# Handing out an expert's four row gathers at once instead of in separate chore slots

## The chip, the cores and the metric

The kernel runs on one core of one Trainium2 chip. The metric is the device time of one execution in microseconds (us); the times given are medians of several executions. A core has five engines, each with a queue of its own, which holds its instructions in the order in which the program emitted them: TensorE (PE in the profile, its weight loads PEld) multiplies matrices, VectorE (DVE) and ScalarE (ACT) work on tiles, GpSimd (POOL) does both some tile work and the indirect DMAs, and SyncE (SP) only issues DMAs. An instruction waits on semaphores for what it needs, and everything behind it in its queue waits with it.

## What is computed

Attention with a sigmoid in place of the softmax, and behind it a mixture of eight experts in which each of 3584 tokens goes to one expert, 448 tokens to each:

```python
scores = q @ k^T / sqrt(64) - log(448);  attn = sigmoid(scores);  x = attn @ v     # 8 x 12 heads, 448 tokens
# routing: the 3584 x 8 logits x @ w_gate in falling order; a token is given to the
# expert of its largest logit that still has room (448 places each)
for e in range(8):
    h = maximum(x[mask_e] @ w1[e], 0)      # 768 -> 1024
    out[mask_e] = h @ w2[e]                # 1024 -> 768
```

## The kernel before, in words

The first part (to about 275 us) computes attention and logits and writes the rows x to a scratch tensor `xs` in HBM. The rest is the eight experts, one after the other. Which expert comes at which step is found by the routing, so "expert 0" to "expert 7" here are steps 0 to 7, not indices of weights.

**Routing** (`Router`, L118 and on). For each step VectorE finds by a 16-step search (L177, 16 steps of about 2 us) the threshold of the next expert to fill, and builds the list of its 448 tokens in `r_idx` (L297). It is a Python generator that emits a piece of itself at each `next(route)`; the list of a step is known to the program as `listed[kx]`. The list of step kx + 1 is built while the expert of step kx multiplies; the routing runs a little faster than the experts, so the lists come earlier and earlier in their expert's predecessor.

**An expert** (`moe`, L667). Its rows must be transposed, since TensorE contracts over partitions. All products are made of three float32r products of high and low parts (high x high, high x low, low x high). First layer: 4 blocks of 2 units of weights, 18 matmuls each (L687, L689, L691); second layer: 3 blocks of 2 units, 24 matmuls each (L722, L724, L726). So there are 14 units an expert, and 288 matmuls. At the start of each unit `stream` (L609) loads the weights of the unit three ahead (SP's queue, L592 and L596) and splits those of the unit two ahead: ScalarE rounds to the high part `wh` (L603), GpSimd subtracts for the low part `wl` (L605; from unit 84 on, so in experts 6 and 7, odd units go to VectorE). After each block of the first layer ScalarE writes the high part `hh` of the hidden layer (L695) and a plain copy (L698), and GpSimd subtracts for the low part `hl` (L699). After each block of the second layer ScalarE copies the result to `yt` (L730).

**The gathers** (`gather`, L623). The 448 rows of an expert come in four blocks of 128, 128, 128 and 64. Each block is one indirect DMA on GpSimd (L625), which reads the rows named by `r_idx` from `xs` into a tile `xr` (12 buffers, shared with the rows of the result).

**The half-turns** (`xturn`, L628). Each block is transposed in two halves of three transposes (L639) into a PSUM tile `tp`, of which there are two. ScalarE rounds it to `xh` (L642), VectorE subtracts for `xl` (L643), and then the PSUM tile is free. Eight half-turns make an expert's input.

**The untransposes** (`untranspose`, L648). Each of the three result blocks is transposed back in four pieces through the same two PSUM tiles (L652, L657); after the last, GpSimd issues the scatter of that block of rows to the output (L660), with a small memset (L659) in front.

**The order around the change** is set by a planner at build time (L754 and on). `clock[0]` is a clock of the program's own, which each matmul moves on by 189 ns (107 ns for the first block of expert 0, whose columns are cut in two); it is no measurement. Three things hang on it:

- The routing's next piece is emitted when the clock has passed the cost of the last piece (constants in L29, plus 150 ns).
- Chores stand in a list with a due time each. When at least 1000 ns (`CHORE_NS`) have passed since the last chore, the first in the list that is due is emitted, between two matmuls. Half-turns, untransposes and (before) gathers are chores.
- When an expert's matmuls are all emitted, `flush` emits in a row whatever the next expert still needs.

`prepare` (L759) is called once for each next expert, at the first matmul at which its list exists, or at the first matmul of its predecessor if the list is older. On the planner's clock, counted from the start of the expert that is running, that is at 47.2, 41.2, 36.1, 31.0, 25.9, 20.8 and 0.2 us for experts 1 to 7 (an expert's matmuls take 54.4 us on it, those of expert 0 55.3). The half-turns are due `lag` after that, block by block 1.5 us apart, where the lag lies between 5 and 14 us and aims at 40 us into the running expert; it is 5 us for experts 1 to 3, 9 us for expert 4 and 14 us for experts 5 to 7.

Because a chore is emitted between matmuls, a gather that is a chore also falls at some place of GpSimd's queue: between the low parts of weights, the low parts of the hidden layer and the scatters that are emitted around it.

Of the kernel before, what the change touches and what calls it, by code (L numbers as in the profile page):

```python
# [338 lines left out]
def moe_attention(tc, q, k, v, w_gate, w1, w2, out):  # L339
# [7 lines left out]
    with contextlib.ExitStack() as ctx:  # L347
# [271 lines left out]
        def blocks():  # L619
            for j in range(4):  # L620
                yield j, min(128, S - 128 * j)

        def gather(kx, j, n):  # L623
            t = xg[kx, j] = xp.tile([128, DM], F32, name="xr", bufs=XR_BUFS)
            nc.gpsimd.indirect_dma_start(out=t[:n], out_offset=None, in_=xs,  # L625
                                         in_offset=bass.IndirectOffsetOnAxis(ap=listed[kx][:n, j:j + 1], axis=0))

        def xturn(kx, j, n, hf, wide):  # L628
            if (j, hf) == (0, 0):
                XH[kx] = (xp.tile([128, ND, S], F32R, name="xh", bufs=2),  # L630
                          xp.tile([128, ND, S], F32R, name="xl", bufs=2))
            xh, xl = XH[kx]
            if wide and hf:
                p = ps_s.tile([128, 2, 512], F32, name="sc")[:, 0]
            else:
                p = ps_t.tile([128, 512], F32, name="tp")
            for i in range(3):
                dd = hf * 3 + i
                nc.tensor.transpose(p[:, i * n:(i + 1) * n], xg[kx, j][:n, dd * 128:(dd + 1) * 128], ident[:n, :n])  # L639
            pv = p[:, :3 * n].rearrange("p (a t) -> p a t", a=3)  # L640
            sl = (slice(None), slice(hf * 3, hf * 3 + 3), slice(j * 128, j * 128 + n))
            nc.scalar.activation(xh[sl], pv, AF.Copy)  # L642
            nc.vector.tensor_tensor(xl[sl], pv, xh[sl].bitcast(F32), OP.subtract)  # L643

        scat, chores = [], []
# [109 lines left out]
        for kx in range(E):  # L755
            turned = kx + 1 == E
            start = clock[0]

            def prepare():  # L759
                t0 = clock[0]  # L760
                lag = max(5000, min(14000, start + 40000 - t0))
                for j, n in blocks():
                    chores.append((t0 + 1500 * j, kx + 1, lambda j=j, n=n: gather(kx + 1, j, n)))
                for j, n in blocks():
                    for hf in range(2):
                        chores.append((t0 + lag + 1500 * j, kx + 1,
                                       lambda j=j, n=n, hf=hf: xturn(kx + 1, j, n, hf, False)))

            def flush(kx):
                for c in [c for c in chores if c[1] <= kx]:  # L770
                    chores.remove(c)
                    c[2]()

            for step, cost in enumerate(moe(kx)):
                clock[0] += cost
                t = clock[0]
                if kx == 0 and step == 35:
                    flush(0)
                if t >= t_route:
                    t_route = t + next(route, 0) + SLACK  # L780
                if not turned and kx + 1 in listed:
                    prepare()
                    turned = True
                if t >= t_chore:
                    c = next((c for c in chores if c[0] <= t), None)
                    if c:
                        chores.remove(c)
                        c[2]()
                        t_chore = t + CHORE_NS
            if not turned:  # L790
                while kx + 1 not in listed:
                    next(route)
                prepare()
            flush(kx + 1)
# [28 lines left out]
```

## Time and profile before

| | us |
|---|---|
| median of 3 runs | 888.54 (888.09 to 889.72) |
| the profiled execution | 887.7 |
| its span, first to last instruction | 885.9 |

The mean granted TensorE clock was 0.986. Busy in the span: TensorE 843.1 us (95%), its weight loads 638.0 (72%), VectorE 534.8 (60%), ScalarE 457.1 (52%), GpSimd 466.1 (53%).

| group | count | busy us | mean ns |
|---|---|---|---|
| L605 low part of weights, GpSimd | 96 | 205.8 | 2153 |
| L699 low part of the hidden layer, GpSimd | 32 | 68.2 | 2133 |
| L625 gather, GpSimd | 32 | 31.9 | 997 |
| L177 search, VectorE | 315 | 123.2 | 441 |

How to read it: a row of the timeline gives the start and length in us, the engine, the line of the kernel, the operation, what it writes and reads, its shape, how many were merged, and in brackets how long the engine had stood idle before it and what ended that. A matmul of 448 columns shows 0.36 us of length, but starts every 0.20 us, because matmuls overlap in the pipeline. "issue" is time in which an engine waited for nothing that the profile shows. A DMA's own row on GpSimd is only its issue; the transfer runs on from there. PEclk is the share of the full clock that TensorE was granted.

### The profile page before, as it was taken

To read this page: it belongs to the slowest core of one execution; us is meant where nothing else is said; L and a number is where in the kernel's file an instruction comes from. 1 tells how busy PE (TensorE), PEld (TensorE's weight loads), DVE (VectorE), ACT (ScalarE), POOL (GpSimd) and SP (SyncE) were. 2 spreads that over 40 slices of the span, in tenths; PEclk is the share of its full clock that TensorE was granted. 3 is DMA by queue.
4 is the path that set the end of the run, shared out by engine and by line. 5 is a ranking of instruction groups with operands and counts; after the bars stand their busy time and mean duration, and the time that the engine had idled before them with its cause. 6 is when DMAs were issued, how large, how long until landed. Compare 5 with 4: busy or idle time off the path is not lost.

```text
span 885.9 us, 16254 instructions
## 1 busy us (share of the span) xinstructions
PE 843.1 (95%) x5507; PEld 638.0 (72%) x5507; DVE 534.8 (60%) x2055; ACT 457.1 (52%) x634; POOL 466.1 (53%) x446
## 2 busy tenths in 40 slices
PE   6999999999998739998999999999999999999996
PEld 3455555455454529987988988888888888989996
DVE  4566555555554988958869779779689521421110
ACT  6777677777774734334424434434434434443431
POOL 9744344444400014845864963873883882852651
PEclk9999999999999969999999999999999999999999
DMA  8876766666612864334443442552551542632511
GB/s 171 167 145 148 147 127 126 129 123 126 130 39 72 262 196 139 118 108 160 127 142 104 149 154 74 170 164 86 162 164 59 188 147 72 219 120 72 193 49 62
DMA packets 203507, 117.57 MB, mean 133 GB/s; under 512 B 143936, under 2 KB 193088, under 8 KB 203424
## 3 DMA queue, kind: packets, MB, share of 16 engines
q1 hardware_dynamic: 190688, 83.03, 36.0%
q0 software_dynamic: 10880, 33.28, 11.9%
q8 instruction: 43, 0.70, 0.3%
q10 hardware_dynamic: 1856, 0.23, 0.2%
q14 instruction: 40, 0.33, 0.1%
HBM read 94.47 MB, written 22.02 MB: 131 GB/s over the span
## 4 chain that ended last, share of the span: by engine, by line
PE 79%; DVE 11%; issue 5%; POOL 3%; DMA 1%; ACT 0%; SPq 0%; POOLq 0%; DVEq 0%
PE tp L455 13%; PE sc L431 11%; PE sc L689 8%; PE sc L687 8%; PE sc L691 8%; PE sc L724 6%; PE sc L726 6%; PE sc L722 6%; DVE r_junk L177 4%; PE tp L461 2%; PE sc L441 2%; PE tp L652 2%; PE tp L639 2%; POOL wl L605 1%; POOL hl L699 1%
## 5 line engine op out<-in xcount | busy, mean ns | idle before, releaser
L605 POOL TENSOR_TENSOR wl<-wr,wh 128x768 fp32r<-128x768 f32 (+1 forms) x96 | 205.8, 2153 | 135.1 <-ACT wh L603 127.4
L421 ACT ACTIVATE at<-sc,bias 128x896 f32<-128x896 f32 x168 | 161.3, 1004 | 66.9 <-PE sc L441 38.4
L381 POOL DMA_DIRECT2D nkq<-in_q_dram x188 | 118.3, 645 | 115.9 <-DVE kqT L406 102.5
L726 PE MATMUL sc<-hh,wl 128*128 128x448 f32 (+2 forms) x400 | 151.5, 379 | 0.0
L691 PE MATMUL sc<-xh,wl 128*128 128x448 f32 (+2 forms) x396 | 146.2, 369 | 0.0
L689 PE MATMUL sc<-xl,wh 128*128 128x448 f32 (+2 forms) x396 | 145.7, 368 | 0.0
L724 PE MATMUL sc<-hl,wh 128*128 128x448 f32 (+2 forms) x400 | 145.5, 364 | 0.2 <-POOL hl L699 0.2
L687 PE MATMUL sc<-xh,wh 128*128 128x448 f32 (+2 forms) x396 | 144.8, 366 | 0.0
L722 PE MATMUL sc<-hh,wh 128*128 128x448 f32 (+2 forms) x400 | 144.0, 360 | 0.0
L177 DVE TENSOR_SCALAR_CACHE_REDUCE r_junk<-r_KE,r_T 128x224 bf16<-128x224 f32 x315 | 123.2, 441 | 0.1
L455 PE MATMUL tp<-at,nv 128*64 128x448 f32 x576 | 118.8, 548 | 0.0
L603 ACT ACTIVATE wh<-wr 128x768 fp32r<-128x768 f32 (+1 forms) x112 | 102.0, 939 | 10.0 <-DMA wr<-in_moe_w_dram 10.0
L699 POOL TENSOR_TENSOR hl<-yt,hh 128x896 fp32r<-128x896 f32 x32 | 68.2, 2133 | 45.8 <-ACT yt L698 44.3
L415 DVE TENSOR_TENSOR kqL<-kqT,kqH 128x896 fp32r<-128x896 f32 (+1 forms) x49 | 52.5, 1073 | 58.5 <-ACT kqH L414 58.3
L695 ACT ACTIVATE hh<-sc 128x896 fp32r<-128x896 f32 x32 | 29.4, 919 | 111.5 <-PE sc L691 108.2
L724 PEld LDWEIGHTS sc<-hl,wh 128*128 128x128 f32 x400 | 75.2, 188 | 7.3 <-issue 1.1
L625 POOL DMA_INDIRECT xr<-xs,r_idx x32 | 31.9, 997 | 92.1 <-ACT wh L603 81.3
L605 DVE TENSOR_TENSOR wl<-wr,wh 128x768 fp32r<-128x768 f32 (+1 forms) x16 | 25.0, 1567 | 91.7 <-ACT wh L603 85.5
L689 PEld LDWEIGHTS sc<-xl,wh 128*128 128x128 f32 x396 | 75.1, 190 | 6.4 <-issue 0.4
L455 PEld LDWEIGHTS tp<-at,nv 128*64 128x64 f32 x576 | 37.1, 136 | 59.1 <-issue 56.3
L687 PEld LDWEIGHTS sc<-xh,wh 128*128 128x128 f32 x396 | 75.4, 190 | 5.7
L722 PEld LDWEIGHTS sc<-hh,wh 128*128 128x128 f32 x400 | 75.6, 189 | 4.6
(157 smaller groups left out, 1328.1 us busy)
## 6 DMA issues: line engine op xcount, KB each, us to landing
wr<-in_moe_w_dram SPq DMA_DIRECT2D x64, 384.0 KB
wr<-in_moe_w_dram SPq DMA_DIRECT2D x48, 512.0 KB
nkq<-in_k_dram SPq DMA_DIRECT2D x192, 56.0 KB
xs<-xr SPq DMA_DIRECT2D x32, 336.0 KB
nkq<-in_q_dram POOLq DMA_DIRECT2D x188, 56.0 KB, 2.7
nv<-in_v_dram SPq DMA_DIRECT2D x92, 96.0 KB
nr<-in_v_dram SPq DMA_DIRECT2D x46, 32.0 KB
xr<-xs,r_idx POOLq DMA_INDIRECT x32, 4.4
```

The lines of the kernel that those rows point to most:

```text
L177: nc.vector.tensor_scalar(junk, KE, T[:, i:i + 1].bitcast(F32), None, OP.is_ge, OP.add, accum_out=cnt[:, i:i + 1])
L381: qn.dma_start(t[o:o + 32, n], rws[x])
L421: nc.scalar.activation(a, p[:, :, :S], AF.Sigmoid, bias=bias, scale=1 / math.sqrt(D))
L455: nc.tensor.matmul(p[j * 64:j * 64 + 64, :S], nat["v", b, g][:, h0 + j, c, :], AT[b, pr, c][:, j, :], start=(c == 0), stop=(c == 2 and pr ...
L603: nc.scalar.activation(hi, raw[u], AF.Copy)
L605: eng.tensor_tensor(lo, raw[u], hi.bitcast(F32), OP.subtract)
L687: nc.tensor.matmul(ph[:, f, lo:hi], wh[:, a, fs], xh[:, dd, lo:hi], start=st, stop=False)
L689: nc.tensor.matmul(ph[:, f, lo:hi], wh[:, a, fs], xl[:, dd, lo:hi], start=False, stop=False)
L691: nc.tensor.matmul(ph[:, f, lo:hi], wl[:, a, fs], xh[:, dd, lo:hi], start=False, stop=en)
L722: nc.tensor.matmul(py[:, d2, :w], wh[:, a, dsl], h1, start=st, stop=False)
L724: nc.tensor.matmul(py[:, d2, :w], wh[:, a, dsl], h2, start=False, stop=False)
L726: nc.tensor.matmul(py[:, d2, :w], wl[:, a, dsl], h1, start=False, stop=(j == 1 and a == 3))
```

## The change

`prepare` calls `gather` itself, four times in a row, where it had put four chores into the list; and the lag's lower bound goes from 5000 to 5500 ns. The four gathers of expert 0 were emitted in a row already (L740) and stay as they are.

```diff
             def prepare():
                 t0 = clock[0]
-                lag = max(5000, min(14000, start + 40000 - t0))
+                lag = max(5500, min(14000, start + 40000 - t0))
                 for j, n in blocks():
-                    chores.append((t0 + 1500 * j, kx + 1, lambda j=j, n=n: gather(kx + 1, j, n)))
+                    gather(kx + 1, j, n)
                 for j, n in blocks():
                     for hf in range(2):
                         chores.append((t0 + lag + 1500 * j, kx + 1,
                                        lambda j=j, n=n, hf=hf: xturn(kx + 1, j, n, hf, False)))
```

## The prediction

> **What bounds the kernel now.** I read the page's span and its chain that ended last, then the waits of TensorE and the busy times over the expert stage.
>
> ```profile
> span 885.9 us, 16254 instructions
> ...
> PE 79%; DVE 11%; issue 5%; POOL 3%; DMA 1%; ACT 0%; SPq 0%; POOLq 0%; DVEq 0%
> ```
>
> TensorE carries 79% of the chain, and GpSimd (POOL) 3%. The experts run from about 330 us to the end. The next view is the busy time of each engine in that stretch (after the length: PE, PEld, DVE, ACT, POOL).
>
> ```profile
> sum 556.00, PE 541.58 PEld 480.59 DVE 339.13 ACT 229.80 POOL 334.74; mean PE 541.58 PEld 480.59 DVE 339.13 ACT 229.80 POOL 334.74
> ```
>
> TensorE is idle for only 14.4 of 556 us, and a part of that is the scatter at the very end. No time can be won where TensorE doesn't wait, and each microsecond that a late operand costs it goes straight into the total. So the question is which of its few waits the gathers cause, and which waits their new place makes. Waits of TensorE from 340 us on (total us, times, longest):
>
> ```profile
> PE tp L639 <- DVE xl L643: 4.9, 5, 1.8
> ...
> PE sc L724 <- POOL hl L699: 0.2, 1, 0.2
> ```
>
> None of these names a gather. The largest belongs to the transposes of the next expert's rows (L639). The small one matters as a warning: at one place GpSimd's low part of the hidden layer (L699) comes just too late, so GpSimd has no slack there.
>
> **What moves.** 28 of the 32 gathers are touched, those of experts 1 to 7; the four of expert 0 stay. Nothing is added or removed: the same 28 indirect DMAs, on the same queue. On GpSimd the first gather of each expert keeps its place; the second to fourth move up, past whatever of L605 (low parts of weights), L699 and the scatters (L660) stood between. SP's queue and DMA traffic in bytes stay as they are. On TensorE no gather issues anything, but the planner hands out one chore slot per microsecond, so the slots that gathers used go to half-turns (xturn: three transposes) and untransposes.
>
> The lag's new lower bound (5.5 for 5.0 us) I cost at nothing. It applies only to experts 1, 2 and 3. Counting the planner's clock through the slots, it holds the first half-turn of experts 2 and 3 where the gathers' slots had put it, to 0.2 us; at expert 1 it moves it from 52.3 to 52.9 us, and three still come before the end.
>
> **Gain: the turn of expert 1.** Its list is ready at 47.2 us of the planner's clock in expert 0, whose matmuls end at 55.3. Before, the last three slots ahead of that (52.9, 54.0 and 55.1) went to gathers, so all eight half-turns fell to the flush at the end. GpSimd, then TensorE there:
>
> ```profile
> 392.46 0.98 POOL L625 DMA_INDIRECT xr<-xs,r_idx  x1
> ...
> 401.34 0.91 POOL L625 DMA_INDIRECT xr<-xs,r_idx  x1 [0.30 <-issue]
> ```
>
> ```profile
> 400.95 0.82 PE L639 MATMUL tp<-ident,xr 128*128 128x128 f32 x6
> 403.58 0.84 PE L639 MATMUL tp<-ident,xr 128*128 128x128 f32 x6 [1.81 <-DVE xl L643]
> 405.27 1.01 PE L639 MATMUL tp<-ident,xr 128*128 128x128 f32 x6 [0.85 <-DVE xl L643]
> 406.99 1.05 PE L639 MATMUL tp<-ident,xr 64*128 64x64 f32 x6 [0.70 <-DVE xl L643]
> 407.96 0.74 PE L687 MATMUL sc<-xh,wh 128*128 128x448 f32 x1
> ```
>
> Two PSUM tiles serve the half-turns, so they go in pairs, each pair waiting until VectorE has read the one before: four rounds in 7.0 us (400.95 to 407.96), the later ones 1.7 us apart. A half-turn among matmuls costs far less, as this row of the chain for expert 7 shows:
>
> ```profile
> 766.91 0.33 PE tp L639 x3
> ```
>
> After the change these three slots go to half-turns. Their rows are there: the page's row for gathers gives the time from issue to landing,
>
> ```profile
> xr<-xs,r_idx POOLq DMA_INDIRECT x32, 4.4
> ```
>
> so with four issues from 392.46 on, 1.28 us apart (rows below), the last lands at about 400.7, the first at 396.9. Two half-turns leave the flush and cost 2 x 0.33 among the matmuls; the third goes one matmul ahead of the flush. Three rounds are left instead of four: 1.7 - 0.7 = 1.0 us gained. The bounds are 0 (VectorE's search steps between the half-turns eat the round) and 4.3 (7.0 less 8 x 0.33, no wait left at all); I take 1.0, since five half-turns still fall to the flush.
>
> This stall has a second price, in the granted clock (columns: stretch, length, busy PE, PEld, DVE, ACT, POOL, then PEclk, DMA share, GB/s):
>
> ```profile
> 401.00:408.00 7.00, 3.64 (x26) 2.57 (x24) 4.32 (x17) 3.84 (x8) 0.94 (x2) 0.93 0.42 146
> 408.00:411.00 3.00, 3.00 (x12) 2.62 (x11) 2.71 (x16) 1.06 (x2) 1.79 (x2) 0.59 0.01 3
> ```
>
> After 7 us in which TensorE was busy for 3.64, the clock fell: 0.59 over the next 3.00 us is 1.2 us lost. With a shorter stall it may not fall. I take one third of it, 0.4 (bounds 0 and 1.2). The Trainium skill (TensorE: Matmul & The Clock Gate, Part 1) says that the clock halves after an idle window of about 3.4 us, the windows running freely. By that rule a stall cut to about 5 us can still hold such a window, so nothing would be gained here; the trace shows a fall in a stretch that was half busy, so idle must not mean empty.
>
> **Price: expert 5, low hidden part.** List 5 comes just before the second layer of expert 4. GpSimd, then the matmul that first reads the last low part:
>
> ```profile
> 646.43 0.99 POOL L625 DMA_INDIRECT xr<-xs,r_idx  x1
> 648.00 2.13 POOL L699 TENSOR_TENSOR hl<-yt,hh 128x896 fp32r<-128x896 f32 x1 [0.57 <-ACT yt L698]
> ...
> 653.92 0.95 POOL L625 DMA_INDIRECT xr<-xs,r_idx  x1 [0.30 <-issue]
> 655.17 0.90 POOL L625 DMA_INDIRECT xr<-xs,r_idx  x1 [0.30 <-issue]
> ```
>
> ```profile
> 652.98 0.36 PE L724 MATMUL sc<-hl,wh 128*128 128x448 f32 x1
> ```
>
> A gather and the gap behind it take 0.98 + 0.30 = 1.28 us. Four in a row from 646.43 end at 646.43 + 3 x 1.28 + 0.90 = 651.2; L699 then ends at 653.3 instead of 650.1, where TensorE wants it at 652.98. The 2.85 us of cover are used up: 0.4 us of stall (bounds 0 and 0.7).
>
> **Price: expert 6.**
>
> ```profile
> 714.00 1.64 POOL L625 DMA_INDIRECT xr<-xs,r_idx  x1 [0.30 <-issue]
> ...
> 719.47 0.91 POOL L625 DMA_INDIRECT xr<-xs,r_idx  x1 [0.16 <-issue]
> 720.40 2.13 POOL L699 TENSOR_TENSOR hl<-yt,hh 128x896 fp32r<-128x896 f32 x1
> ```
>
> ```profile
> 722.58 0.47 PE L724 MATMUL sc<-hl,wh 128*128 128x448 f32 x1 [0.16 <-POOL hl L699]
> ```
>
> All four gathers already stand ahead of this L699, and TensorE waits for it. Only one swaps with a weight's low part; the gap before it grows from 0.16 to 0.30: 0.1 us.
>
> **Price: expert 7.** List 7 is early, and its gathers are issued at the start of expert 6, in front of expert 5's four scatters. Before, only the first stood ahead of those; now all four do. GpSimd behind the scatters, then TensorE's load of that low part of weights (unit 4):
>
> ```profile
> 760.96 0.98 POOL L625 DMA_INDIRECT xr<-xs,r_idx  x1 [0.30 <-issue]
> 761.97 2.14 POOL L699 TENSOR_TENSOR hl<-yt,hh 128x896 fp32r<-128x896 f32 x1
> 764.05 1.84 POOL L605 TENSOR_TENSOR wl<-wr,wh 128x768 fp32r<-128x768 f32 x1
> ```
>
> ```profile
> 766.14 0.19 PEld L691 LDWEIGHTS sc<-xh,wl 128*128 128x128 f32 x1
> ```
>
> L605 ended at 765.89, 0.25 us before it was wanted. The second gather (760.96) was ahead of it already; the third and fourth come in front now: 2 x 1.28 = 2.56, less 0.25, is 2.3 us of TensorE stall (bounds 1.5, if gaps close up, and 3.6, if both moved gathers take 1.64 as the one at 714.00 did). Nothing later gives this back, because TensorE has hardly any waits left to absorb it. VectorE's two passes of weights' low parts nearby:
>
> ```profile
> 755.07 0.96 DVE L605 TENSOR_TENSOR wl<-wr,wh 128x768 fp32r<-128x768 f32 x1 [7.84 <-ACT wh L603]
> 762.06 4.66 DVE L605 TENSOR_TENSOR wl<-wr,wh 128x768 fp32r<-128x768 f32 x1 [6.03 <-issue]
> ```
>
> The same pass takes 0.96 alone and 4.66 beside GpSimd's L699 and L605. The Trainium skill (SBUF — State Buffer, Who interferes with whom) explains that a two-input VectorE instruction meets GpSimd's reads at a shared port. By it the second pass, now beside scatters, would be short; that moves no term of the sum.
>
> **No price, as I see it: experts 2, 3 and 4.** For expert 4 the low part at 584.79 moves behind three gathers:
>
> ```profile
> 584.79 2.42 POOL L605 TENSOR_TENSOR wl<-wr,wh 128x1024 fp32r<-128x1024 f32 x1
> ```
>
> ```profile
> 595.37 0.45 PE L726 MATMUL sc<-hh,wl 128*128 128x448 f32 x1
> ```
>
> It ends at 584.79 + 3.8 + 2.42 = 591.0, and is wanted at 595.4. Without this cover it would cost up to 3.8. Experts 2 and 3 have more slack by the same count. Expert 3's half-turns come in another phase to VectorE's search steps; there TensorE waited once:
>
> ```profile
> 532.79 0.55 PE L639 MATMUL tp<-ident,xr 128*128 128x128 f32 x3 [0.89 <-DVE xl L643]
> ```
>
> Three untransposes now go ahead of them and fill such a wait; I take 0, between -0.9 and +0.9.
>
> **Sum.** -1.0 - 0.4 + 0.4 + 0.1 + 2.3 = +1.4 us. The profiled execution took 887.7, so 889.1 there; the median before is 888.54, 0.8 above the profiled one, so **889.9**. By the bounds of the terms it lies between about 889.0 and 891.0, leaving the far ends to the rivals. About 0.2% (1.8 us) is what a measurement of this kernel can tell from no change.
>
> **Rivals.**
>
> *Slower: the stall at unit 4 of expert 6 drags the clock down.* TensorE stands for 2.3 us; if that puts it below what the gate wants, the next 3 us cost 1.2 more, as at 408. Longer gathers (1.64) add 0.3 or so: 891.4. It decides once that stall weighs on the gate as the turn at 401 to 408 did, where TensorE was idle for 3.4 of 7.0 us in three pieces. For it: 2.3 us in one piece is longer than any of those. Against it: dense matmuls stand right before and behind. By the rule of the Trainium skill's clock gate page (TensorE: Matmul & The Clock Gate, Part 1) it would not happen, 2.3 us being less than its window of 3.4.
>
> *GpSimd catches up.* The scatters are issued tighter than before, or L605 comes early enough, and the 2.3 vanish: -0.9, 887.6. Against it: GpSimd has no gap in that stretch that I could take away.
>
> *Faster: the turn runs clean.* Of the 7.0 + 1.2 us at expert 1 only 8 x 0.33 are left and the stall at expert 7 halves: -5.5 + 1.7, some 884.7; a form half-way gives 886.6. Against it: five half-turns still in the flush, with two PSUM tiles.
>
> *It does nothing.* If the later gathers each wait for something else, such as their tile, the order is moot: 888.5.
>
> **Chances.** Forecast 0.50 (0.28 of it within 0.2%, 0.22 beyond), slower rival 0.20 (0.19 beyond), GpSimd catches up 0.15 (0.03 faster), clean turn 0.08 (0.07 faster), nothing 0.07. That makes faster 0.10, the same 0.49, slower 0.41. The range leaves out the clean turn and the worst of the slow side: 887.2 to 892.0.
>
> **What would show it.** Right: four gathers in a row on GpSimd for every expert; at expert 1 three pairs of half-turns between the last L726 and the first L687, not four; a TensorE wait of about 2.3 us on L605 at the fifth unit of expert 6, and one of 0.4 on L699 at expert 4. Wrong: no wait on L605, a turn of expert 1 as long as before, or new waits on VectorE at experts 2 and 3.

## The result, and the profile after

| | before | after |
|---|---|---|
| median, us | 888.32 (887.57 to 889.72, 4 runs) | 898.01 (896.17 to 898.99, 4 runs) |
| the profiled execution | 887.7 | 896.17 |
| its span | 885.9 | 894.4 |

The ratio is 1.0104 (95% interval 1.0088 to 1.0119). The medians lie 9.7 us apart, and the ratio makes it 9.2 us: slower either way, and outside the range of the prediction. First the head of the page after the change, its span and its chain:

```profile
span 894.4 us, 16255 instructions
...
PE 75%; DVE 12%; issue 6%; POOL 5%; DMA 1%; ACT 1%; SPq 0%; POOLq 0%; DVEq 0%
```

TensorE's share of the chain fell from 79 to 75%; VectorE's rose from 11 to 12% and GpSimd's from 3 to 5%. Now the waits of TensorE from 340 us on:

```profile
PE tp L639 <- DVE xl L643: 9.8, 8, 3.3
PE sc L691 <- POOL wl L605: 2.5, 1, 2.5
...
PE sc L724 <- POOL hl L699: 0.4, 2, 0.2
```

The wait on L605 was predicted (2.3 us), and so was a small one on L699. The first line was not: the half-turns waited 4.9 us for VectorE before, and now wait 9.8, once for 3.3. These are the rows of TensorE, in order of time, that stood still longer than before:

```profile
532.42 0.55 PE L639 MATMUL tp<-ident,xr 128*128 128x128 f32 x3 [1.85 <-DVE xl L643]
...
654.05 0.47 PE L724 MATMUL sc<-hl,wh 128*128 128x448 f32 x1 [0.17 <-POOL hl L699]
...
668.69 0.55 PE L639 MATMUL tp<-ident,xr 128*128 128x128 f32 x3 [3.31 <-DVE xl L643]
671.48 0.55 PE L639 MATMUL tp<-ident,xr 128*128 128x128 f32 x3 [1.00 <-DVE xl L643]
...
728.26 0.47 PE L724 MATMUL sc<-hl,wh 128*128 128x448 f32 x1 [0.24 <-POOL hl L699]
...
774.69 0.47 PE L691 MATMUL sc<-xh,wl 128*128 128x448 f32 x1 [2.51 <-POOL wl L605]
```

Read by stage, with the start of each stage or unit (its first L687 or L722 row) in both traces, the whole difference comes out as a sum:

| stretch | before | after | lead or lag at its end | change in it |
|---|---|---|---|---|
| last unit of expert 0 starts | 395.64 | 395.93 | +0.29 | +0.29 (ahead of the change) |
| expert 1 starts (its turn) | 407.96 | 407.22 | -0.74 | -1.03 |
| its second layer starts | 439.32 | 438.98 | -0.34 | +0.40 |
| second layer of expert 2 starts | 507.64 | 507.25 | -0.39 | -0.05 |
| second layer of expert 3 starts | 577.09 | 577.75 | +0.66 | +1.05 |
| second layer of expert 4 starts | 645.99 | 646.73 | +0.74 | +0.08 |
| its fourth unit starts | 662.09 | 663.26 | +1.17 | +0.43 |
| expert 5 starts | 681.03 | 686.62 | +5.59 | +4.42 |
| expert 6 starts | 750.44 | 756.13 | +5.69 | +0.10 |
| its second layer starts | 783.58 | 792.04 | +8.46 | +2.77 |
| last unit of expert 7 starts | 875.05 | 883.51 | +8.46 | 0 |

The largest entry, +4.42, lies where the half-turns of expert 5 wait for VectorE. What held VectorE is found by going back on its own queue to the last instruction that is longer than in the trace of before. Before, the search's first step (L210, an operation on 128x3 numbers) and the first `xl` of expert 5:

```profile
652.91 0.23 DVE L210 TENSOR_SCALAR r_T<-c_kk,r_J 128x3 int32<-128x3 int32 x1
...
662.49 0.55 DVE L643 TENSOR_TENSOR xl<-tp,xh 128x384 fp32r<-128x384 f32 x1
```

After, the same two, and the operation ahead of L210:

```profile
653.40 0.21 DVE L208 TENSOR_SCALAR r_J<-r_PF,r_J 128x1 int32<-128x1 int32 x1
653.65 5.08 DVE L210 TENSOR_SCALAR r_T<-c_kk,r_J 128x3 int32<-128x3 int32 x1
...
668.09 0.55 DVE L643 TENSOR_TENSOR xl<-tp,xh 128x384 fp32r<-128x384 f32 x1
```

L210 took 5.08 us for 0.23, and what stands behind it on VectorE came 4.85 us later for it (the `xl` 5.60 later in all, of which 0.74 is the lag that was there already). Two half-turns had filled the two PSUM tiles by then, and the third stood until the first `xl` had freed one. And this is what GpSimd did meanwhile, after the change:

```profile
647.14 0.99 POOL L625 DMA_INDIRECT xr<-xs,r_idx  x1
...
650.95 0.90 POOL L625 DMA_INDIRECT xr<-xs,r_idx  x1 [0.30 <-issue]
651.87 2.13 POOL L699 TENSOR_TENSOR hl<-yt,hh 128x896 fp32r<-128x896 f32 x1
653.94 4.75 POOL L605 TENSOR_TENSOR wl<-wr,wh 128x1024 fp32r<-128x1024 f32 x2
659.74 2.40 POOL L605 TENSOR_TENSOR wl<-wr,wh 128x1024 fp32r<-128x1024 f32 x1 [1.04 <-ACT wh L603]
```

One L699 and two L605 in a row without a gap, to 653.94 + 4.75 = 658.69; L210 ended at 653.65 + 5.08 = 658.73. Before, L210 at 652.91 fell on a gather, which ran on GpSimd from 652.63 to 653.61:

```profile
650.08 2.42 POOL L605 TENSOR_TENSOR wl<-wr,wh 128x1024 fp32r<-128x1024 f32 x1
652.63 0.98 POOL L625 DMA_INDIRECT xr<-xs,r_idx  x1
```

The gathers had broken up GpSimd's run of two-input operations there; handed out in a row, they leave that run closed.

At expert 3 the same instruction takes 1.62 us at 527.83 (before: 1.25 at 528.24) and ends within 0.04 us of a low part of weights on GpSimd both times. In both traces it stands ahead of that expert's first `xl`. What differs is what lies between the two. Before, the `xl` follows at once:

```profile
528.24 1.25 DVE L210 TENSOR_SCALAR r_T<-c_kk,r_J 128x3 int32<-128x3 int32 x1
529.40 0.54 DVE L643 TENSOR_TENSOR xl<-tp,xh 128x384 fp32r<-128x384 f32 x1
```

After, the whole next search step, 2.3 us long, comes first:

```profile
527.83 1.62 DVE L210 TENSOR_SCALAR r_T<-c_kk,r_J 128x3 int32<-128x3 int32 x1
529.48 0.45 DVE L177 TENSOR_SCALAR_CACHE_REDUCE r_junk<-r_KE,r_T 128x224 bf16<-128x224 f32 x1
...
531.82 1.01 DVE L643 TENSOR_TENSOR xl<-tp,xh 128x384 fp32r<-128x384 f32 x2
```

The wait of 0.89 us became 1.85. So the +1.05 at expert 3 comes mostly from the planner's order, and only a little (0.37 us of L210) from the hold; experiments 4 and 5 give 0.8 of it with L210 free.

### The profile page after: what moved, and what is told of

Same layout as the page of the kernel before. It is cut to its first block, busy times and chain, and to the rows that moved or that the text cites. A ratio compares the mean times of both kernels' runs of the same rounds, so it can differ in the third digit from the quotient of the medians.

```text
span 894.4 us, 16255 instructions
## 1 busy us (share of the span) xinstructions
PE 844.4 (94%) x5507; PEld 638.5 (71%) x5507; DVE 535.4 (60%) x2055; ACT 457.8 (51%) x634; POOL 465.9 (52%) x446
## 4 chain that ended last, share of the span: by engine, by line
PE 75%; DVE 12%; issue 6%; POOL 5%; DMA 1%; ACT 1%; SPq 0%; POOLq 0%; DVEq 0%
PE tp L455 13%; PE sc L431 11%; PE sc L689 8%; PE sc L687 8%; PE sc L691 7%; PE sc L726 6%; PE sc L724 6%; PE sc L722 5%; DVE r_junk L177 4%; PE tp L461 2%; PE sc L441 2%; PE tp L652 2%; POOL wl L605 2%; PE tp L639 2%; POOL hl L699 1%
## 5 line engine op out<-in xcount | busy, mean ns | idle before, releaser
L605 POOL TENSOR_TENSOR wl<-wr,wh 128x768 fp32r<-128x768 f32 (+1 forms) x96 | 205.7, 2154 | 139.6 <-ACT wh L603 132.3
L687 PE MATMUL sc<-xh,wh 128*128 128x448 f32 (+2 forms) x396 | 144.9, 366 | 0.0
L722 PE MATMUL sc<-hh,wh 128*128 128x448 f32 (+2 forms) x400 | 144.0, 360 | 0.0
L177 DVE TENSOR_SCALAR_CACHE_REDUCE r_junk<-r_KE,r_T 128x224 bf16<-128x224 f32 x315 | 123.3, 441 | 0.1
L699 POOL TENSOR_TENSOR hl<-yt,hh 128x896 fp32r<-128x896 f32 x32 | 68.3, 2133 | 48.7 <-ACT yt L698 47.2
L691 PEld LDWEIGHTS sc<-xh,wl 128*128 128x128 f32 x396 | 75.2, 190 | 7.9 <-POOL wl L605 2.9
L687 PEld LDWEIGHTS sc<-xh,wh 128*128 128x128 f32 x396 | 75.6, 191 | 5.5
L722 PEld LDWEIGHTS sc<-hh,wh 128*128 128x128 f32 x400 | 75.6, 189 | 4.3
```

The source lines that it names most:

```text
L177: nc.vector.tensor_scalar(junk, KE, T[:, i:i + 1].bitcast(F32), None, OP.is_ge, OP.add, accum_out=cnt[:, i:i + 1])
L605: eng.tensor_tensor(lo, raw[u], hi.bitcast(F32), OP.subtract)
L687: nc.tensor.matmul(ph[:, f, lo:hi], wh[:, a, fs], xh[:, dd, lo:hi], start=st, stop=False)
L691: nc.tensor.matmul(ph[:, f, lo:hi], wl[:, a, fs], xh[:, dd, lo:hi], start=False, stop=en)
L722: nc.tensor.matmul(py[:, d2, :w], wh[:, a, dsl], h1, start=st, stop=False)
```

## The experiments

Theory A: VectorE's L210 is held as long as GpSimd runs two-input operations back to back, the gathers were the gaps, and the half-turns of expert 5 pay. Against it stand two others: that the half-turns are late because of the planner's phase and the order on TensorE (more half-turns and untransposes close together), whatever L210 does; and that GpSimd's later low parts cost the time in general, spread over all experts. All ratios are to runs of the kernel before on the same chip in the same group; the medians of before there were 887.9, 888.3 and 888.66. The groups of experiments 1 to 4, 5 to 8 and 9 to 12 each ran together. A gain or loss in us is worked out from the ratio; the medians can differ from it by half a microsecond.

**1 and 2. The whole change without one expert.** In the first, expert 5's gathers stay chores; in the second, those of expert 7. The diff, to the kernel before, is that of the first; the second has `(1, 2, 3, 4, 5, 6)`. The lag's bound is 5500 for the experts listed and 5000 for the others.

```diff
-                lag = max(5000, min(14000, start + 40000 - t0))
+                at_once = kx + 1 in (1, 2, 3, 4, 6, 7)
+                lag = max(5500 if at_once else 5000, min(14000, start + 40000 - t0))
                 for j, n in blocks():
-                    chores.append((t0 + 1500 * j, kx + 1, lambda j=j, n=n: gather(kx + 1, j, n)))
+                    if at_once:
+                        gather(kx + 1, j, n)
+                    else:
+                        chores.append((t0 + 1500 * j, kx + 1, lambda j=j, n=n: gather(kx + 1, j, n)))
```

> The change, except that the gathers of expert 5 stay separate chores. Theory A (port): with gathers again between GpSimd's low parts, the search step at L210 in expert 4 takes 0.2 us instead of 5.1, the turn of expert 5 loses its waits on VectorE (3.3 and 1.0), and the run is 4.9 us faster than the change, about 893 us, 4.5 to 5 above before. Rival B (only GpSimd's queue is late, and VectorE's delay is a consequence of something else in the change, such as the phase of the half-turns from expert 3 on): at most the 0.2 us of L699 come back, about 897.5.

Measured: 892.69 us, ratio 1.0062 (1.0039 to 1.0085). TensorE's waits in it:

```profile
PE tp L639 <- DVE xl L643: 5.4, 6, 1.8
PE sc L691 <- POOL wl L605: 2.5, 1, 2.5
```

> The change, except that the gathers of expert 7 stay separate chores. The queue theory of the prediction (third and fourth gather and four scatters ahead of the low part of unit 4): the wait of 2.5 us on L605 in expert 6 goes, and the run is 2.7 us faster than the change, about 895. If that wait only uncovers another behind it: less than 1 us.

Measured: 893.57 us, ratio 1.0060 (1.0037 to 1.0083). The wait on L605 is gone, and that of 3.2 us on `xl` is there. Without expert 5 the loss falls by about 0.4%, without expert 7 also (each known to 0.2%); these are two separate causes in two places, and most of the loss is not spread over all experts. Without expert 7 more came back than the 2.7 us expected, within what the two intervals leave open.

**3. Expert 5 alone** (`in (5,)`).

> The kernel before, except that the gathers of expert 5 are handed out at once. Theory A (port): the place of these four gathers alone makes two L605 follow L699 with no gap, L210 is held for about 5 us, and the run is 5 us slower than before, about 893.3. Rival B: at most 0.3 us slower than before, since nothing of the half-turns' order differs.

Measured: 893.48 us, ratio 1.0065 (1.0047 to 1.0083). L210 in it:

```profile
650.74 5.10 DVE L210 TENSOR_SCALAR r_T<-c_kk,r_J 128x3 int32<-128x3 int32 x1
```

This expert's gathers alone cost 5.8 us, more than half of the whole loss, with L210 held as in the whole change.

**4. The whole change, with L210 through PSUM.** The operation is split into two: the first does what L195 does in the later search steps and writes to PSUM, the second has the form of L214 and reads one input from PSUM. VectorE has one instruction more; the order on TensorE and on GpSimd is that of the whole change. If order or phase on TensorE made the loss, nothing would move.

```diff
-                nc.vector.tensor_scalar(T, K.kk[:, 1], nJ, None, OP.bitwise_xor)
+                if pe:
+                    nc.vector.tensor_scalar(T, K.kk[:, 1], nJ, None, OP.bitwise_xor)
+                else:
+                    nc.vector.tensor_scalar(X[:, 8:11], K.kk[:, 1], K.c0[:, 1:2], None, OP.bitwise_xor)
+                    nc.vector.scalar_tensor_tensor(T, nJ.to_broadcast([128, 3]), 0, X[:, 8:11],
+                                                   OP.logical_shift_left, OP.bitwise_xor)
```

> The whole change, with one thing else: the first search step's thresholds (L210) are made by two VectorE instructions that read one operand from PSUM, of the forms that L195 and L214 have and that are never long in the traces, instead of one that reads and writes only SBUF. It adds 0.1 to 0.2 us of VectorE work per expert. Theory A (port): the step is no longer held, the waits of expert 5's half-turns go, about 4.9 us come back, and up to 1 more at expert 3, so 892 to 893. Rival C (the gathers' transfers or GpSimd's late low parts make the half-turns late): no change from the change, about 898.

Measured: 890.39 us, ratio 1.0026 (1.0009 to 1.0043). The new pair in place of L210 (the lines behind it move by 5), and GpSimd beside it:

```profile
651.24 0.22 DVE L213 TENSOR_SCALAR rt<-c_kk,c_c 128x3 int32<-128x3 int32 x1
651.49 0.16 DVE L214 SCALAR_TENSOR_TENSOR r_T<-r_J,rt 128x3 int32<-128x3 int32 x1
```

```profile
649.58 2.13 POOL L704 TENSOR_TENSOR hl<-yt,hh 128x896 fp32r<-128x896 f32 x1
651.65 4.74 POOL L610 TENSOR_TENSOR wl<-wr,wh 128x1024 fp32r<-128x1024 f32 x2
```

At the same place, beside the same closed run of GpSimd, the pair took 0.22 and 0.16 us. TensorE's longest wait on `xl` is 1.1 us instead of 3.3, and that of 2.5 us on the low part of weights stays. So the order on TensorE, which is unchanged here, is not the cause of what went away. About three quarters of the loss hung on this one small instruction, more than expected (892 to 893). The second layer of expert 2, where expert 3's half-turns lie, and the first layer of expert 3 still take 0.8 us longer together than in experiment 5, which has the order of before and the same L210; so there the order costs something even with L210 free.

**5. The same edit alone, on the kernel before.** This is the control for experiment 4.

> The kernel before with the search step of L210 written to go through PSUM (the same edit as in e4_port), its gathers as before. Theory A (L210 is held at VectorE's and GpSimd's shared port): before, L210 is long once, 1.25 us at expert 3, so the edit is worth at most the 0.89 us wait of the half-turns there: 0 to -1. Then e4_port's remaining loss against this kernel is expert 7's stall (2.5 to 2.8) less expert 1's gain (0.7). Rival (the edit makes the search faster as such, whatever the gathers do): -5 us or more here too, as it took 7.6 from the whole change.

Measured: 886.82 us, ratio 0.9985 (0.9972 to 0.9997). So the edit is worth 1.3 us without the change too (a little more than expected), and about 7 us with it (1.0104 against 1.0026). In its profile the second layer of expert 2 takes 36.68 us instead of 37.63, and expert 3's half-turns no longer wait there. It is the only kernel here that is measurably faster than the one before.

**6 and 11. What could be kept of the change.** L210 through PSUM as in 4, with the gathers at once for experts 1 to 6, and for experts 2 to 6 (the diffs are those of 1 and 4 together).

> The whole change for experts 1 to 6, expert 7's gathers left as chores, and L210 through PSUM. If the three causes add (port, low part of weights at expert 6, turn of expert 1), the two losses are gone and the gain at expert 1 stays: -0.4 to -1.5 against the kernel before, that is 886.8 to 887.9 where before is 888.3. If the losses have another part in common (GpSimd's order as such), it stays 1 us or more above.

Measured: 888.05 us, ratio 1.0002 (0.9987 to 1.0018), just above what was expected and no gain.

> e6_best without expert 1: gathers at once for experts 2 to 6, L210 through PSUM, expert 1's turn in four rounds as before. If e6_best lost its gain to the clock that falls at the three-round turn of expert 1, this one stands 1 us or so better, near e5_before_port: 886.8 to 887.5. If it lost it among experts 2 to 6, it is again at 888 or above.

Measured: 888.11 us, ratio 0.9996 (0.9986 to 1.0006). That is between the two forecasts, and the intervals of experiments 5, 6 and 11 overlap, so the medians do not settle where the gain of 5 went. The profiles show one place: in 11, the second layer of expert 2 takes 38.03 us (507.67 to 545.70) against 36.68 in 5 (504.83 to 541.51), with two waits for `xl`, 0.8 us together, that 5 does not have; the first layer of expert 3, out of which three untransposes have moved forward, gives 0.65 of that back. The 0.70 that is left is the same in 6 and 0.8 in 4, and is about what the two waits come to: the search step stands between L214 and the first `xl` there too, as it does not in 5. In all these runs the lag's bound moved together with the gathers, so which of the two shifts that order was not tested.

**7. Expert 1 alone** (`in (1,)`).

> The kernel before with only expert 1's gathers at once. Turn of expert 1 in three rounds: second layer of expert 1 and all behind it 0.3 (clock falls again at 408) to 1.9 us (it does not) early; nothing else moves: 886.4 to 888.0 where before is 888.3. If the gain is given back (expert 3's half-turns are late again): 888.3.

Measured: 887.14 us, ratio 0.9993 (0.9980 to 1.0007): 0.6 us better (1.2 between the medians), and not told apart from nothing.

**8. The whole change with a small instruction between.** A memset of one element stands in front of each L605 of expert 4, so that GpSimd's two-input operations no longer follow each other directly.

```diff
             eng = nc.vector if u < 2 or (u >= W_DVE and u % 2) else nc.gpsimd
+            if units[u][0] == 4 and eng is nc.gpsimd:
+                nc.gpsimd.memset(spacer, 0.0)
```

> The whole change, with a one-element memset (0.1 us or less of GpSimd) in front of each low part of weights (L605) emitted in expert 4, so that L699 and the L605s do not stand back to back. If the hold of L210 ends at any other instruction of GpSimd, it is short again (up to 0.6 us, to the end of L699), the 3.3 us wait is gone, and the time falls by 4.5 to 5 us against the whole change, to about 893.3. If it ends only when GpSimd's queue has a real gap, or the next two-input operation gets the port again first, L210 stays at 5 us and the time at 898.

Measured: 898.86 us, ratio 1.0119 (1.0097 to 1.0141), as bad as the whole change. GpSimd and L210 in it:

```profile
652.09 2.12 POOL L701 TENSOR_TENSOR hl<-yt,hh 128x896 fp32r<-128x896 f32 x1
654.15 0.09 POOL L606 MEMSET spacer<- 1x1 f32 x1
654.20 2.40 POOL L607 TENSOR_TENSOR wl<-wr,wh 128x1024 fp32r<-128x1024 f32 x1
656.53 0.09 POOL L606 MEMSET spacer<- 1x1 f32 x1
656.58 2.40 POOL L607 TENSOR_TENSOR wl<-wr,wh 128x1024 fp32r<-128x1024 f32 x1
658.92 0.09 POOL L606 MEMSET spacer<- 1x1 f32 x1
```

```profile
653.82 5.22 DVE L210 TENSOR_SCALAR r_T<-c_kk,r_J 128x3 int32<-128x3 int32 x1
```

Each memset starts before its forerunner has ended (654.15 against 652.09 + 2.12 = 654.21), and the next L607 starts before the memset has ended. L210 got through at 653.82 + 5.22 = 659.04, when GpSimd first stood idle. So a short instruction was no gap. A gather, with the 0.16 us of idle time in front of it, was one: in the kernel before, L210 at expert 3 ended at 529.49, between the end of an L605 (527.05 + 2.40 = 529.45) and a gather at 529.61.

**9. Expert 3 alone** (`in (3,)`).

> The kernel before with only expert 3's gathers at once. If the wait before expert 3's first half-turn grows because L210 now stands ahead of the xl that frees the PSUM tile (the prediction's phase, taken as 0): the wait goes from 0.9 to about 1.8 and expert 3 starts 1.7 us late against expert 2's second layer; 889.3 to 890.0 where before is 888.3. If that loss came from expert 2's gathers instead, nothing moves: 888.3.

Measured: 890.6 us, ratio 1.0017 (1.0006 to 1.0029), +1.5 us. The wait is there (1.83 us in its profile, 0.89 before), with the search step between L210 and the first `xl` as in the whole change, and in that execution the clock fell behind it. In this view (columns as in the prediction) the first row holds the wait:

```profile
530.00:533.50 3.50, 1.77 (x11) 1.27 (x8) 3.33 (x17) 0.49 (x1) 0.60 (x1) 1.00 0.59 184
533.50:536.50 3.00, 2.90 (x13) 2.62 (x14) 2.86 (x17) 1.86 (x3) 0.00 (x0) 0.70 0.00 0
```

**10. Expert 7 alone** (`in (7,)`).

> The kernel before with only expert 7's gathers at once. By the prediction's term: the fifth unit of expert 6 waits 2.5 us on L605 and takes 2.7 longer: 891.0. By the prediction's slower rival (clock falls after the stall): that unit takes 4.3 longer, as in one profile of the runs above, and the time is 892.6; a mixture lies between. If the stall is made up for later: 888.3.

Measured: 891.07 us, ratio 1.0028 (1.0015 to 1.0041), +2.5 us, the forecast's term. In the profiled execution, 892.0 us, the rival's mechanism came on top:

```profile
766.00:769.00 3.00, 0.50 (x3) 0.13 (x1) 0.00 (x0) 2.45 (x3) 3.00 (x3) 1.00 0.17 43
769.00:772.00 3.00, 2.98 (x10) 2.64 (x11) 0.56 (x1) 0.49 (x1) 3.00 (x2) 0.55 0.48 152
```

Behind the stall the clock stood at 0.55, and the unit took 9.01 us (765.94 to 774.95) instead of 4.66 before and 7.41 in the profile of the whole change (771.62 to 779.03), where the clock did not fall.

**12. L210 as one two-input operation in SBUF.** The whole change, with L210 in the form of L214, which is never long, but with both inputs and the output in SBUF.

```diff
-                nc.vector.tensor_scalar(T, K.kk[:, 1], nJ, None, OP.bitwise_xor)
+                nc.vector.scalar_tensor_tensor(T, nJ.to_broadcast([128, 3]), 0, K.kk[:, 1],
+                                               OP.logical_shift_left, OP.bitwise_xor)
```

> The whole change, with L210 as one two-input operation (scalar_tensor_tensor, the form of L214) that still reads and writes SBUF alone. If what is held is the place (an operation with both its inputs in SBUF meets GpSimd's port), it is long again and the time stays at 898. If it is the form (tensor_scalar takes a mode that needs the port for itself), it is short, the 3.3 us wait goes and the time falls by 4.5 us or more, to 893.5 or below; with the loss at expert 3 gone too, to 890.4 as in e4_port.

Measured: 897.97 us, ratio 1.0109 (1.0094 to 1.0125), no better than the whole change. L210 in it, beside an L700 and two L606 that ran from 650.87 to 657.69:

```profile
652.62 5.10 DVE L210 SCALAR_TENSOR_TENSOR r_T<-r_J,c_kk 128x3 int32<-128x3 int32 x1
```

So the form of L210 does not save it as long as everything that it reads and writes lies in SBUF, and the way through PSUM (4) does. That both operands lie in SBUF is not enough for a hold, though. L177 reads a tile and one threshold per partition from SBUF and writes SBUF, and L195, like the first instruction of the pair in 4, reads such a pair from SBUF and writes PSUM; neither is ever long. In the trace after the change 113 of the L177 and 37 of the L195 ran wholly beside GpSimd's subtractions, in 0.43 to 0.45 and in 0.18 us, no longer than the others. These two ran beside the L605 that started at 659.74:

```profile
660.13 0.18 DVE L195 TENSOR_SCALAR rt<-c_kk,r_J 128x3 int32<-128x3 int32 x1
661.10 0.44 DVE L177 TENSOR_SCALAR_CACHE_REDUCE r_junk<-r_KE,r_T 128x224 bf16<-128x224 f32 x1
```

What it is in L210's first form that is held, no run here tells apart: its result in SBUF, or something else in which it differs from L177.

**Together.** The four parts measured alone add up: expert 1 -0.6, expert 3 +1.5, expert 5 +5.8, expert 7 +2.5 make +9.2, and the whole change measured +9.2 by its ratio. Each part is known to 1 or 2 us, and it holds the clock falls that came with it; experts 2, 4 and 6 were not measured alone.

## Why the prediction was wrong

**The step that failed** is one sentence of the term for expert 7. The prediction quoted two rows in which the same VectorE pass takes 0.96 us alone and 4.66 beside GpSimd's L699 and L605, named the shared port, and closed with "that moves no term of the sum". It asked only what becomes of that one pass, and had that right: after the change it took 0.96 us, at 767.74, beside scatters. It did not ask which other VectorE instructions lie beside GpSimd's runs once the gathers no longer break them up, and who waits for those. Experiments 3, 4 and 12 show what belonged there: L210, a VectorE operation of 0.23 us held for 5.1, with the half-turns' `xl` behind it in the queue, and 4.42 us of TensorE's time. The Trainium skill (SBUF — State Buffer, Who interferes with whom) says that a VectorE instruction with two SBUF inputs meets a GpSimd instruction that reads SBUF, and that one with at most one SBUF input does not, outside the modes that use both ports. Of the two-tensor form, 5.10 us with both inputs in SBUF (12) and 0.16 with one in PSUM (4) agree. A number per partition can't count as such an input, or L177 and L195 would be long too. Whether L210 in its first form, with one tensor and one number per partition, was held by such a mode no run here shows.

A second, smaller step failed with it: the phase of expert 3's half-turns against the search steps, bounded by -0.9 to +0.9 and taken as 0. It was +1.05. The prediction worked out that the first half-turn keeps its place to 0.2 us on the planner's clock; the order in which half-turn and search step were emitted changed all the same.

Point by point, with the terms as predicted and as the table of stages has them:

- **Expert 1, -1.0 and -0.4.** The turn gained 1.03, by the step foreseen: three slots with single half-turns (398.58, 400.14, 401.69), then two pairs and a single one:

```profile
403.45 1.01 PE L639 MATMUL tp<-ident,xr 128*128 128x128 f32 x6 [1.07 <-DVE xl L643]
405.17 0.87 PE L639 MATMUL tp<-ident,xr 128*128 128x128 f32 x6 [0.71 <-DVE xl L643]
406.89 0.40 PE L639 MATMUL tp<-ident,xr 64*128 64x64 f32 x3 [0.85 <-DVE xl L643]
```

The clock was mis-sized, and in sign. It fell again, and lower than the 0.59 of before:

```profile
408.00:411.00 3.00, 3.00 (x10) 2.61 (x10) 2.86 (x18) 0.73 (x2) 1.84 (x2) 0.50 0.01 3
```

So the term was +0.4, not -0.4. The first unit of expert 1 took 5.8 to 6.7 us in all eight profiles with this shorter turn; with four rounds it took 5.4 to 5.8 in four and 4.4, without a fall, in two. The shorter stall did not spare the clock.

- **Experts 2, 3 and 4, no price.** GpSimd's low parts there cost nothing, as argued. At expert 3 the untransposes did go ahead of the half-turns, as foreseen, but on VectorE a whole search step went ahead of the first `xl` too, and the wait grew by 0.96 us.
- **Expert 5, +0.4 for the low hidden part.** 0.43 in the stretch with that wait: right (its own rows, 653.3 against 652.98, give 0.3). The half-turns of the same expert cost 4.42 more and had no term.
- **Expert 6, +0.1.** 0.10: right.
- **Expert 7, +2.3.** The wait was 2.51 and cost 2.77: right in its place and cause.
- **The slower rival**, a clock that falls behind the stall, was priced somewhat low (1.2; it measured 1.6), and its weight was too low. In six profiles with the 2.5 us stall the fifth unit of expert 6 took 7.41 us in two and 9.0 in four. Behind the 3.3 us stall at expert 4 the unit took 10.97 in one and 12.3 to 12.5 in four. The profiled execution of the whole change is one in which neither fell, which fits its place at the low end of the four runs (896.17 of 896.17 to 898.99), 1.8 below their median. The prediction cited the Trainium skill (TensorE: Matmul & The Clock Gate, Part 1), whose idle window of about 3.4 us would have ruled the fall out; the rows of experiments 9 and 10, with waits of 1.83 and 2.51 us and a clock of 0.70 and 0.55 behind them, show that it happens.

The sum: 1.4 predicted, + 4.42 for L210 at expert 5, + 1.05 for the order at expert 3, + 0.8 for the clock at expert 1, + 0.47 at expert 7, + 0.29 that lay ahead of the change, is 8.43; the two profiled executions differ by 8.47. The rest, to 9.7 between medians, is put down to clock falls, by inference.

What stays open: why the clock falls behind a stall in one execution and not in another, what exactly in L210's first form is held, and whether the gathers or the lag shift the order at expert 3.

## What to carry to other kernels

When an edit closes gaps on one engine, look for what used those gaps on its neighbour: list every operation of the other engine that the trace shows at two lengths, find what lies beside the long ones, and ask where each will lie after the edit. A tiny operation counts as much as a big one if a queue stands behind it; here 0.23 us of work became 5.1 us of delay. Rewritten as two steps through PSUM, this operation stepped out of the way altogether (0.38 us for the pair), and that edit alone gained 1.3 us where the reordering lost 9.

## What the runs showed of the hardware that was not expected

- L210 was not let in between GpSimd instructions that stand back to back: it waited through three of them (5.08 us), and a 0.09 us memset between them did not let it in either (5.22 us).
- The operation on a single column was not held: L208, 128x1 with its inputs in SBUF, took 0.21 us at 653.40 in the middle of the L699 at 651.87, and L210, 128x3, started 0.25 us later and was held.
- In two of the eight profiles with expert 6's gathers at once (6 and 8), VectorE stood idle for 3.9 us at 716 and at 722 us, with nothing in the profile that it waited for, and TensorE then waited 1.0 us for the next VectorE instruction. The cause was not looked for.
